# Attention feeding a gated feed-forward layer on one core: larger first loads, another order of the first unit, and the second normalisation beside two gate and value blocks

## The chip, the cores and the metric

The kernel runs on one core of a Trainium2 chip. A core has a matrix engine (TensorE, PE), a vector engine (VectorE, DVE), a scalar engine (ScalarE, ACT), GpSimd (POOL) and SyncE (SP), and 16 DMA engines that move data between the device memory and the on-chip memory. Each engine runs its own list of instructions in order and waits on semaphores of the others. The metric is the device time of one execution in microseconds.

## The reference

`q`, `k`, `v` are 8 batches x 12 heads x 448 positions x 64, in float32. The attention has no softmax: the scores are rectified and squared. Its result, 3584 tokens x 768, goes through a root-mean-square normalisation and a gated feed-forward layer of width 1536.

```python
scores = scale * np.matmul(q, k.transpose(0, 1, 3, 2))
attn = np.maximum(scores, 0.0) ** 2 / S
x = np.matmul(attn, v)                      # heads side by side: 3584 x 768
xn = x / np.sqrt(np.mean(x * x, axis=-1, keepdims=True) + 1e-06) * rms_g
g = xn @ w_gate
out = (g * (1.0 / (1.0 + np.exp(-g))) * (xn @ w_val)) @ w_out
```

## The kernel before

All matrix products are in bfloat16. The loads, issued by GpSimd, turn float32 into bfloat16 on the way. GpSimd keeps at most eight loads under way; a further one is issued when the one eight places ahead of it has landed.

A unit of attention is four heads of one batch, two pairs; a batch has three units (`ND = 3`), so unit `m` belongs to batch `m // 3`. For a unit, queries and keys are transposed so that the head dimension lies on the partitions (`QT`, `KT`). The keys of a pair come in three blocks of 128 (`NCH`) and a rest of 64 that both pairs share in one tile (`kx`, "late keys"); so a unit has seven score slots, 0 to 6. `scores` (line 318) makes the scores of a slot for both heads of a pair (TensorE), rectifies them (ScalarE, line 344) and squares them (VectorE, line 311). `attend` multiplies with the values into `psAV`, ScalarE scales the sums into `xT` and VectorE squares those into `xn`.

Batch 0 is done in two parts of its query positions, `US = ((0, 3), (3, 7))`: 192 and 256 positions. Its functions are `first_q`, `first_k` (transposes on TensorE, copies on VectorE, lines 255 and 277), `last_keys` (late keys), `part_scores` (line 351; four tiles a unit, slots (0,1), (2,3), (4,5), (6)), `part_attend` and `part_gates`. `late` collects the squares, to be issued afterwards (`flush`). From batch 2 on, the keys are transposed by DMAs that SyncE issues (`turn_by_dma`, line 285): three blocks and the late keys for a batch. Queries of batches 2 and 3 (`pr == 1`) are transposed by TensorE in `transposes` (line 190), from batch 4 on by DMA.

`norm` sums the squares over the model dimension by a product with ones (`psSS`), takes the root (ScalarE, line 492) and puts small VectorE steps on a list `bg`: two or four reciprocals (line 503), six scalings (line 506, one for each block of 128 of the model dimension), and last a call that makes the gate and value pieces available. `step()` does the next of these, `steps(n)` does n, `drain()` all. A piece on the list `pieces` is a block of products: for batch 0 the gate product of two column blocks (`psG`, line 530, followed by the sigmoid step `sig` on ScalarE, line 548) or the value product (`psV`, line 530, then the multiplication into `hT`, line 553). `piece(n)` runs the next n of them.

ScalarE loads a table of functions when it changes between the root and the sigmoid step (1.28 us each in the timeline). The PSUM memory is split into two buffers for scores (`psS`) and four that all other products share in turn (`rot`). `warm(k)` issues k products of ones with 448 columns (`psW`, line 303) whose result is not used; `warm_tile()` takes a buffer for them.

The opening is written out by hand, lines 138 to 168 for the loads and 679 to 747 for the work: first part of batch 0, its `norm`, second part with pieces of the first between, its `norm`, then the first slots of batch 1. From line 748 a loop over units takes over and fills with pieces by their costs; outputs follow from `outproj`.

Of the kernel before, what the change touches and what calls it, by code (L numbers as in the profile page):

```python
# [15 lines left out]
def kernel(  # L16
# [37 lines left out]
    def cols(h):  # L54
        return slice(US[h][0] * HALF, US[h][1] * HALF)
# [41 lines left out]
    def load_q0(h, h0=0, h1=H):  # L97

        u0, u1 = US[h]
        nc.gpsimd.dma_start(  # L100
            out=q_t[0][:HALF, h0:h1, u0:u1],
            in_=q[0, h0:h1].rearrange("h (p u) d -> p h u d", u=NU)[:, :, u0:u1],
        )
# [7 lines left out]
    def load_k(b, h0=0, h1=H):  # L111
        src = k[b, h0:h1, 0:XT0]
        form = "h (p c) d -> p h c d" if b < 2 else "h (p c) d -> p c h d"
        dst = k_t[b][:, h0:h1] if b < 2 else k_t[b][:]
        nc.gpsimd.dma_start(out=dst, in_=src.rearrange(form, c=NCH))  # L115

    def load_kx(b):
        nc.gpsimd.dma_start(out=kx_t[b][:], in_=k[b, :, XT0:S].rearrange("h p d -> p h d"))
# [19 lines left out]
    q_tile(0)  # L138
    k_tile(0)
    v_tile(0)  # L140
    load_q0(0, 0, 2)
    load_k(0, 0, 2)
    ident = const_pool.tile([P, P], BF16, name="ident", tag="ident")
    masks.make_identity(nc, ident[:])
    load_k(0, 2, 4)
    load_q0(0, 2, 12)
    load_k(0, 4, 8)
    load_kx(0)
    load_v(0, 0, 4)
    load_vx(0)  # L150
    load_k(0, 8, 12)
# [89 lines left out]
    def first_q(h, t, pairs=(0, 1)):  # L241

        u0, u1 = US[h]
        n, i0 = len(pairs), pairs[0]
        ps = psum.tile([P, n, u1 - u0, HALF], BF16, name="psQ", tag="rot", bufs=4)
        for i in pairs:
            for u in range(u0, u1):
                turn(
                    ps[:, i - i0, u - u0, :],
                    lambda hh: q_t[0][:, 4 * t + 2 * i + hh, u, :],  # L250
                    0,
                    HALF,
                )
        j = 2 * t + i0
        nc.vector.tensor_copy(out=QT[0][:, j : j + n, u0:u1, :HALF], in_=ps[:])

    def first_k(t, pairs=(0, 1)):

        w, n, i0 = (S if t else XT0), len(pairs), pairs[0]
        ps = psum.tile([P, n, w], BF16, name="psK", tag="rot", bufs=4)  # L260
        for i in pairs:
            for c in range(NCH):
                turn(
                    ps[:, i - i0, c * P : (c + 1) * P],
                    lambda hh: k_t[0][:, 4 * t + 2 * i + hh, c, :],
                    0,
                    P,
                )
            if t:
                turn(  # L270
                    ps[:, i, XT0:S],
                    lambda hh: kx_t[0][:, 4 * t + 2 * i + hh, :],
                    0,
                    XK,
                )
        j = 2 * t + i0
        nc.vector.tensor_copy(out=KTt[0][:, j : j + n, :w], in_=ps[:])
# [9 lines left out]
    def last_keys(m):  # L287

        b, t = divmod(m, ND)
        ps = psum.tile([P, 2, XK], BF16, name="psX", tag="rot", bufs=4)  # L290
        for i in range(2):
            turn(ps[:, i, :], lambda hh: kx_t[b][:, 4 * t + 2 * i + hh, :], 0, XK)
        nc.vector.tensor_copy(out=KTt[b][:, 2 * t : 2 * t + 2, XT0:S], in_=ps[:])
# [4 lines left out]
    def warm_tile():  # L298
        W["ps"] = psum.tile([P, S], FP32, name="psW", tag="rot", bufs=4)

    def warm(k):
        for _ in range(k):
            nc.tensor.matmul(  # L303
                out=W["ps"][:], lhsT=ones_bf[:, :P], rhs=ones_bf[:], start=True, stop=True
            )
# [45 lines left out]
    def part_scores(h, t, tiles, k=0, late=None):  # L351

        u0, u1 = US[h]
        w = (u1 - u0) * HALF
        qt, kt = QT[0], KTt[0]
        for x in tiles:
            warm(k)
            n = len(PARTS[x])
            ps = psum.tile([P, 2, 512], FP32, name="psS", tag="psS")
            for y, s in enumerate(PARTS[x]):  # L360
                if s < 2 * NCH:
                    i, c = divmod(s, NCH)
                    todo = [(2 * t + i, slice(0, P), slice(c * P, (c + 1) * P))]
                else:
                    todo = [
                        (2 * t + i, slice(i * XK, (i + 1) * XK), slice(XT0, S))
                        for i in range(2)
                    ]
                for j, rows, keys in todo:
                    for hh in range(2):  # L370
                        prt = slice(hh * D, (hh + 1) * D)
                        nc.tensor.matmul(  # L372
                            out=ps[rows, hh, y * w : (y + 1) * w].rearrange(
                                "k (u x) -> k u x", x=HALF
                            ),
                            lhsT=kt[prt, j, keys],
                            rhs=qt[prt, j, u0:u1, :HALF],
                            start=True,
                            stop=True,
                        )  # L380
            r = rpool.tile([P, 1024], BF16, name="r", tag="r")
            r = r[:, : 2 * n * w].rearrange("p (h x) -> p h x", h=2)
            nc.scalar.activation(out=r, in_=ps[:, :, : n * w], func=ACT.Relu)  # L383
            square(r, late)
            for y, s in enumerate(PARTS[x]):
                R[h, t, s] = r[:, :, y * w : (y + 1) * w]

    def part_attend(h, t):
        w = (US[h][1] - US[h][0]) * HALF
        acc = [psum.tile([P, w], FP32, name="psAV", tag="rot", bufs=4) for _ in range(2)]  # L390
        for s in range(2 * NCH + 1):
            r = R.pop((h, t, s))
            if s < 2 * NCH:
                i, c = divmod(s, NCH)
                todo = [(i, slice(0, P), v_t[0][:, 4 * t + 2 * i : 4 * t + 2 * i + 2, c])]
            else:
                c = NCH
                todo = [
                    (
                        i,  # L400
                        slice(i * XK, (i + 1) * XK),
                        vx_t[0][:, 4 * t + 2 * i : 4 * t + 2 * i + 2],
                    )
                    for i in range(2)
                ]
            for i, rows, v in todo:
                for hh in range(2):
                    nc.tensor.matmul(  # L408
                        out=acc[i][hh * D : (hh + 1) * D, :],
                        lhsT=v[rows, hh, :],  # L410
                        rhs=r[rows, hh, :],
                        start=(c == 0),
                        stop=(c == NCH),
                    )
        evacuate(0, t, [(slice(i, i + 1), acc[i][:]) for i in range(2)], cols(h))
# [245 lines left out]
    def piece(n=1):  # L661
        for _ in range(n):
            pieces.pop(0)[1]()

    def steps(n):
        for _ in range(n):
            step()
# [5 lines left out]
    def flush(late):  # L673
        while late:
            late.pop(0)()
# [1 line left out]
    N = B * ND  # L677
    late: list = []
    warm_tile()
    warm(8)  # L680
    big(0, 0)
    first_q(0, 0, (0,))
    first_k(0, (0,))
    warm(1)
    part_scores(0, 0, (0,), late=late)
    warm(2)
    first_q(0, 0, (1,))
    first_k(0, (1,))
    flush(late)
    part_scores(0, 0, (1, 2))  # L690
    last_keys(0)
    first_k(1)
    first_q(0, 1)
    part_scores(0, 0, (3,))
    warm_tile()
    for t in range(1, ND):
        part_scores(0, t, (0,))
        warm(1)
        part_scores(0, t, (1,))
        part_attend(0, t - 1)  # L700
        if t + 1 < ND:
            first_k(t + 1)
            first_q(0, t + 1)
            warm_tile()
        part_scores(0, t, (2, 3))
    first_q(1, 0)
    first_q(1, 1)
    warm_tile()
    warm(2)
    part_attend(0, ND - 1)  # L710
# [1 line left out]
    norm(0, cols(0), lambda: part_gates(0, (0, 2, 4, 6)))  # L712
    drain()
    warm_tile()
    part_scores(1, 0, (0, 1, 2, 3), 2)
    warm(7)
    warm_tile()
    piece(2)
    part_scores(1, 1, (0, 1))
    part_attend(1, 0)  # L720
    piece(1)
    part_scores(1, 1, (2, 3))
    first_q(1, 2)
    piece(1)
    part_scores(1, 2, (0, 1))
    part_attend(1, 1)
    piece(1)
    part_scores(1, 2, (2, 3))
    transposes(HP - 1)
    transposes(HP)  # L730
    last_keys(ND)
    piece(1)
    part_attend(1, 2)
    prefetch_v(0, ND - 1)
    transposes(HP + 1)
    warm_tile()
    warm(2)
    norm(0, cols(1), lambda: part_gates(1, (0, 2, 4, 6)))
    scores(ND, (0, 1), late=late)
    piece(1)  # L740
    steps(4)
    piece(1)
    scores(ND, (2, 3), late=late)
    drain()
    flush(late)
    for h in range(2):
# [60 lines left out]
```

## Time and profile before

| | us |
|---|---|
| median of 3 runs | 472.72 (472.03, 472.72, 484.08) |
| the profiled execution's own time | 475.79 |
| its span, first to last instruction | 474.0 |
| TensorE busy (97% of the span) | 459.7 |
| VectorE, ScalarE busy (54% each) | 254.1, 256.6 |
| GpSimd busy (14%) | 67.8 |

The difference between the profiled execution's own time and its span, 1.79 us, lies before the first and after the last instruction. TensorE's clock is granted in steps by the chip: the profile shows 1.00 or 0.50 of full speed. A busy TensorE at 0.50 does half as much. The loads of the opening, from the list of DMA issues with their times:

| load, heads | KB | issued | landed |
|---|---|---|---|
| queries 0-2 | 48 | 1.26 | 4.59 |
| keys 0-2 | 96 | 1.96 | 5.10 |
| keys 2-4 | 96 | 3.22 | 6.10 |
| queries 2-12 | 240 | 3.94 | 8.72 |
| keys 4-8 | 192 | 4.66 | 9.73 |
| late keys | 96 | 5.41 | 10.84 |
| values 0-4 | 192 | 6.17 | 11.70 |
| keys of batch 2 | 576 | 40.47 | 61.55 |

The KB are those that the profile gives (bytes as written).

### The profile page before, as it was taken

The page shows a single profiled execution, that of the slowest core. Times are in us where ns is not written, and L with a number is a line of the kernel's source. Part 1 is how long each engine was busy: PE and PEld are TensorE (multiplying, and loading weights), DVE is VectorE, ACT ScalarE, POOL GpSimd, SP SyncE. Part 2 cuts the span into 40 slices and gives each one's busy share as a digit, 9 for nine tenths or more (in the row PEclk, how much of TensorE's full clock was granted, in tenths as well). Part 3 has the DMA queues.
Part 4 walks back from the last instruction along what each step waited for, and adds up shares of the span by engine and source line. Part 5 has one row for each costly group of instructions (what it writes and reads, how often), then busy time and mean ns, then how long its engine had stood idle before and what let it go on. Part 6 is the DMA issues. An engine that isn't in the chain of part 4 may idle for free.

```text
span 474.0 us, 8047 instructions
## 1 busy us (share of the span) xinstructions
PE 459.7 (97%) x3276; PEld 240.7 (51%) x3276; DVE 254.1 (54%) x455; ACT 256.6 (54%) x378; POOL 67.8 (14%) x73
## 2 busy tenths in 40 slices
PE   6998899999999999999999999999999999999997
PEld 2556556654454454444445554444445555555564
DVE  2566777885448344955557435855566435522211
ACT  2567768955564567746565447646565444222111
POOL 9535210621040006100300002000000000000000
PEclk8579899999999999999999999999999999999999
DMA  9999999999999629920295548000001120000022
GB/s 100 195 195 192 183 157 130 179 124 133 44 126 183 174 73 132 147 36 1 26 119 134 140 121 88 2 0 1 1 17 68 66 84 2 0 1 0 35 100 100
DMA packets 134196, 42.79 MB, mean 90 GB/s; under 512 B 114576, under 2 KB 134160, under 8 KB 134160
## 3 DMA queue, kind: packets, MB, share of 16 engines
q0 software_dynamic: 97072, 24.38, 62.2%
q1 hardware_dynamic: 36944, 17.80, 17.5%
q8 instruction: 25, 0.41, 0.4%
q14 instruction: 11, 0.09, 0.1%
q10 hardware_dynamic: 144, 0.10, 0.1%
HBM read 48.76 MB, written 11.01 MB: 126 GB/s over the span
## 4 chain that ended last, share of the span: by engine, by line
PE 81%; DMA 6%; ACT 5%; DVE 5%; issue 2%; SPq 1%; POOL 1%; ACTq 0%; POOLq 0%
PE psO L617 21%; PE psG L575 20%; PE psV L589 20%; PE psS L335 6%; PE psAV L437 5%; DMA KT<-kld 4%; PE psW L303 2%; ACT r L344 2%; PE psSS L484 1%; PE psAV L408 1%; DVE r L311 1%; PE psS L372 1%; DMA out_dram<-ost 1%; ACT r L383 1%; DVE xn L506 1%
## 5 line engine op out<-in xcount | busy, mean ns | idle before, releaser
L311 DVE TENSOR_TENSOR r<-r 128x896 bf16<-128x896 bf16 (+4 forms) x171 | 103.9, 615 | 96.1 <-ACT r L344 87.5
L344 ACT ACTIVATE r<-psS 128x896 bf16<-128x896 f32 x147 | 128.0, 924 | 24.3 <-PE psS L335 24.2
L617 PE MATMUL psO<-wo_sb,hT 128*128 128x384 bf16 x672 | 113.2, 326 | 0.4 <-DVE hT L596 0.4
L575 PE MATMUL psG<-xn,wg_sb 128*128 128x448 bf16 x504 | 109.4, 353 | 0.2 <-DVE xn L506 0.2
L589 PE MATMUL psV<-xn,wv_sb 128*128 128x448 bf16 x504 | 109.2, 353 | 0.0
L583 ACT ACTIVATE sig<-psG 128x448 bf16<-128x448 f32 x84 | 45.7, 546 | 89.4 <-PE psG L575 87.2
L617 PEld LDWEIGHTS <-hT 128*128 128x128 bf16 x672 | 64.2, 98 | 47.0 <-issue 5.1
L596 DVE TENSOR_TENSOR hT<-sig,psV 128x448 bf16<-128x448 bf16 x84 | 51.7, 616 | 58.4 <-PE psV L589 56.9
L589 PEld LDWEIGHTS <-wv_sb 128*128 128x128 bf16 x504 | 47.9, 98 | 47.8 <-issue 4.9
L575 PEld LDWEIGHTS <-wg_sb 128*128 128x128 bf16 x504 | 48.0, 98 | 47.2 <-issue 4.0
L633 ACT COPY ost<-psO 128x384 f32<-128x384 f32 x28 | 13.4, 479 | 67.6 <-PE psO L617 50.4
L335 PE MATMUL psS<-QT,KT 64*128 64x448 bf16 (+1 forms) x336 | 44.8, 360 | 2.2 <-ACT r L344 1.8
L635 DVE COPY ost<-psO 128x384 f32<-128x384 f32 x27 | 15.0, 555 | 31.5 <-PE psO L617 31.4
L506 DVE SCALAR_TENSOR_TENSOR xn<-xT,g_sb,rstd 128x448 bf16<-128x448 bf16 (+2 forms) x54 | 31.5, 628 | 0.3
L121 POOL DMA_DIRECT2D vld<-in_v_dram x9 | 8.9, 986 | 156.4 <-PE psAV L437 154.4
L454 ACT ACTIVATE xT<-psAV 128x448 bf16<-128x448 f32 (+2 forms) x54 | 24.3, 503 | 10.3 <-PE psAV L408 5.4
L437 PE MATMUL psAV<-r,vld 128*64 128x448 bf16 x252 | 27.8, 357 | 0.0
L503 DVE RECIPROCAL rstd<-rstd 128x112 f32<-128x112 f32 (+2 forms) x32 | 25.0, 822 | 4.4 <-ACT rstd L492 4.4
L335 PEld LDWEIGHTS <-KT 64*128 64x128 bf16 (+1 forms) x336 | 11.6, 96 | 28.9 <-issue 27.3
L383 ACT ACTIVATE r<-psS 128x768 bf16<-128x768 f32 (+3 forms) x24 | 18.8, 830 | 13.7 <-PE psS L372 13.5
L455 DVE TENSOR_TENSOR xn<-xT 128x896 bf16<-128x896 bf16 (+2 forms) x27 | 15.5, 573 | 11.3 <-ACT xT L454 11.3
L115 POOL DMA_DIRECT2D kld<-in_k_dram x11 | 16.5, 1496 | 24.3 <-DMA KT<-kld 20.7
(53 smaller groups left out, 274.4 us busy)
## 6 DMA issues: line engine op xcount, KB each, us to landing
out_dram<-ost SPq DMA_DIRECT2D x55, 192.0 KB, 1.9
qld<-in_q_dram POOLq DMA_DIRECT2D x7, 672.0 KB, 20.1
kld<-in_k_dram POOLq DMA_DIRECT2D x7, 576.0 KB, 17.2
vld<-in_v_dram POOLq DMA_DIRECT2D x7, 576.0 KB, 7.0
wo_sb<-in_moe_w_out_dram POOLq DMA_DIRECT2D x3, 768.0 KB, 34.7
vxld<-in_v_dram POOLq DMA_DIRECT2D x16, 96.0 KB, 7.2
wg_sb<-in_moe_w_gate_dram POOLq DMA_DIRECT2D x4, 384.0 KB, 13.8
wv_sb<-in_moe_w_val_dram POOLq DMA_DIRECT2D x4, 384.0 KB, 15.0
```

The lines of the kernel that those rows point to most:

```text
L311: nc.vector.tensor_tensor(out=r, in0=r, in1=r, op=ALU.mult)
L335: nc.tensor.matmul(out=ps[rows, hh, :S].rearrange("k (u x) -> k u x", u=NU), lhsT=kt[prt, j, keys], rhs=qt[prt, j, :, b % 2 * HALF : (b % ...
L344: nc.scalar.activation(out=r, in_=ps[:, :, :S], func=ACT.Relu)
L437: nc.tensor.matmul(out=acc[i][hh * D : (hh + 1) * D, :], lhsT=w[rows, hh, :], rhs=r[rows, hh, :], start=(c == 0), stop=(c == NCH),)
L454: nc.scalar.mul(out=xt[:, i, sl], in_=acc, mul=inv_attn)
L503: nc.vector.reciprocal(out=rstd[:, cs], in_=rstd[:, cs])
L506: nc.vector.scalar_tensor_tensor(out=xn[:, kt, sl], in0=xt[:, kt, sl], scalar=g_sb[:, kt : kt + 1], in1=rstd[:, :w], op0=ALU.mult, op1=ALU ...
L575: nc.tensor.matmul(out=ps[:], lhsT=wg_sb[:, kt, fb * P : (fb + 1) * P], rhs=xn[:, kt, :], start=(kt == 0), stop=(kt == KT - 1),)
L583: nc.scalar.activation(out=sig[:, :S], in_=ps[:], func=ACT.Silu)
L589: nc.tensor.matmul(out=ps[:], lhsT=wv_sb[:, kt, fb * P : (fb + 1) * P], rhs=xn[:, kt, :], start=(kt == 0), stop=(kt == KT - 1),)
L596: nc.vector.tensor_tensor(out=HT[pr, fb][:, :, e * HALF : (e + 1) * HALF], in0=st["sig"][:, :S].rearrange("p (u x) -> p u x", u=NU), in1=p ...
L617: nc.tensor.matmul(out=ps[:], lhsT=HT[pr, fk][:, u, :], rhs=wo_sb[:, fk, o * OW : (o + 1) * OW], start=(fk == 0), stop=(fk == FT - 1),)
```

## The change

Three things change, all in the part written by hand. The first loads of queries and of keys take four heads each instead of two, the late keys are loaded third, and the remaining queries after keys 4 to 8. In the first unit all transposes of both pairs come first, then tiles 0 and 1 of the scores, then the late keys and tiles 2 and 3. In the first part two dummy products between tiles go, and all three `first_q(1, t)` are done at its end. Around the first `norm` there are fewer dummies, one tile of scores and one value piece stand in another order, and one gate and one value piece fewer run before the second `norm`, so that two pairs of them run behind it, among `steps`. The number of dummies falls from 42 to 39; all other TensorE instructions are the same in number.

```diff
-    load_q0(0, 0, 2)
-    load_k(0, 0, 2)
+    load_q0(0, 0, 4)
+    load_k(0, 0, 4)
     ident = const_pool.tile([P, P], BF16, name="ident", tag="ident")
     masks.make_identity(nc, ident[:])
-    load_k(0, 2, 4)
-    load_q0(0, 2, 12)
+    load_kx(0)
     load_k(0, 4, 8)
-    load_kx(0)
+    load_q0(0, 4, 12)
     load_v(0, 0, 4)
...
     warm_tile()
-    warm(8)
+    warm(10)
     big(0, 0)
-    first_q(0, 0, (0,))
+    first_q(0, 0)
     first_k(0, (0,))
+    first_k(0, (1,))
+    warm_tile()
+    part_scores(0, 0, (0,), late=late)
     warm(1)
-    part_scores(0, 0, (0,), late=late)
+    part_scores(0, 0, (1,), late=late)
+    last_keys(0)
+    flush(late)
     warm(2)
-    first_q(0, 0, (1,))
-    first_k(0, (1,))
-    flush(late)
-    part_scores(0, 0, (1, 2))
-    last_keys(0)
+    part_scores(0, 0, (2, 3))
     first_k(1)
     first_q(0, 1)
-    part_scores(0, 0, (3,))
     warm_tile()
+    warm(1)
     for t in range(1, ND):
-        part_scores(0, t, (0,))
-        warm(1)
-        part_scores(0, t, (1,))
+        part_scores(0, t, (0, 1))
         part_attend(0, t - 1)
...
-    first_q(1, 0)
-    first_q(1, 1)
+    for t in range(ND):
+        first_q(1, t)
     warm_tile()
     warm(2)
     part_attend(0, ND - 1)
...
     norm(0, cols(0), lambda: part_gates(0, (0, 2, 4, 6)))
     drain()
     warm_tile()
-    part_scores(1, 0, (0, 1, 2, 3), 2)
-    warm(7)
+    part_scores(1, 0, (0, 1), 2)
+    warm(1)
+    part_scores(1, 0, (2,), 2)
+    warm(1)
     warm_tile()
-    piece(2)
+    piece(1)
+    part_scores(1, 0, (3,))
+    piece(1)
     part_scores(1, 1, (0, 1))
     part_attend(1, 0)
     piece(1)
     part_scores(1, 1, (2, 3))
-    first_q(1, 2)
     piece(1)
     part_scores(1, 2, (0, 1))
     part_attend(1, 1)
-    piece(1)
-    part_scores(1, 2, (2, 3))
     transposes(HP - 1)
     transposes(HP)
+    part_scores(1, 2, (2, 3))
     last_keys(ND)
-    piece(1)
-    part_attend(1, 2)
-    prefetch_v(0, ND - 1)
     transposes(HP + 1)
     warm_tile()
     warm(2)
+    part_attend(1, 2)
+    prefetch_v(0, ND - 1)
+    warm(3)
     norm(0, cols(1), lambda: part_gates(1, (0, 2, 4, 6)))
     scores(ND, (0, 1), late=late)
     piece(1)
-    steps(4)
+    steps(2)
     piece(1)
-    scores(ND, (2, 3), late=late)
+    steps(2)
+    scores(ND, (2,), late=late)
+    piece(1)
+    steps(2)
+    scores(ND, (3,), late=late)
+    piece(1)
     drain()
```

## The prediction

> **What bounds the kernel now.** I read the page's slices first, then the busy time by stage, the timeline of TensorE's waits, and the chain in order of time.
>
> ```profile
> PE   6998899999999999999999999999999999999997
> ...
> PEclk8579899999999999999999999999999999999999
> DMA  9999999999999629920295548000001120000022
> GB/s 100 195 195 192 183 157 130 179 124 133 44 126 183 174 73 132 147 36 1 26 119 134 140 121 88 2 0 1 1 17 68 66 84 2 0 1 0 35 100 100
> ```
>
> A slice is 11.85 us. TensorE is full from slice 5 on; it is idle, or clocked below full, only in the first five. There the DMA engines are full too, near 195 GB/s. The busy time by stage sharpens this (columns: TensorE, weight loads, VectorE, ScalarE, GpSimd, granted clock, DMA share, GB/s):
>
> ```profile
> 0.00:8.30 8.30, 5.01 (x27) 1.79 (x27) 1.06 (x4) 2.09 (x2) 7.17 (x15) 1.00 0.74 71
> 8.30:28.80 20.50, 18.66 (x212) 10.59 (x213) 10.01 (x24) 10.47 (x18) 12.69 (x16) 0.50 1.57 191
> 28.80:56.10 27.30, 24.17 (x315) 16.21 (x314) 18.92 (x44) 21.46 (x32) 10.57 (x12) 1.00 1.62 191
> 56.10:59.50 3.40, 3.23 (x14) 1.91 (x14) 3.40 (x9) 1.69 (x3) 0.14 (x1) 0.50 1.97 176
> 59.50:83.80 24.30, 23.17 (x276) 14.64 (x275) 17.96 (x39) 18.82 (x27) 1.50 (x2) 1.00 1.54 144
> 83.80:474.00 390.20, 385.45 (x2434) 195.56 (x2434) 202.72 (x338) 202.04 (x299) 35.78 (x29) 1.00 0.65 74
> ```
>
> After 83.8 us TensorE idles 4.75 of 390 us: whatever moves the start of that stage moves the end by as much. Before it, TensorE idles 9.6 us (the differences of the first two columns) and has the clock at 0.50 for 23.9 us. The timeline shows the waits that the change touches, in brackets, and the last one before the full stage:
>
> ```profile
> 8.77 0.37 PE L190 MATMUL psQ<-ident,qld 64*64 64x64 bf16 x6 [1.98 <-DMA qld<-in_q_dram]
> ...
> 41.93 0.61 PE L372 MATMUL psS<-QT,KT 64*128 64x256 bf16 x8 [1.06 <-DVE QT L255]
> ...
> 54.60 0.25 PE L190 MATMUL psX<-ident,kxld 64*64 64x64 bf16 x4 [0.60 <-ACT sig L548]
> ...
> 60.19 1.47 PE L530 MATMUL psV<-xn,wv_sb 128*128 128x256 bf16 x12 [0.73 <-ACT sig L548]
> ...
> 83.82 0.55 PE L335 MATMUL psS<-QT,KT 64*128 64x448 bf16 x4 [0.25 <-DMA KT<-kld]
> ```
>
> The last is what I build on. At 83.82 the scores of the third batch need the third block of its transposed keys, which SyncE's transposing DMA brings. The chain goes through it:
>
> ```profile
> 63.00 2.38 SPq L285
> 65.38 0.05 issue
> 65.43 18.34 DMA KT<-kld
> 83.77 0.05 issue
> 83.82 0.55 PE psS L335 x4
> ```
>
> That DMA was issued at 65.43, behind the first two (61.64, 63.00), and the first waited for the key load that landed at 61.55. That load was issued at 40.47, as soon as the load eight places ahead of it on GpSimd's queue had landed (39.92): the loads keep a full queue, whatever TensorE does. So at this place TensorE already waits 0.25 us for the stream: being there earlier gains nothing by itself.
>
> **The change part by part.** U is the profiled execution: span 474.0, time 475.79, so 1.79 around it; the median is 472.72, 3.07 lower, and I carry that difference over unchanged.
>
> *First loads.* Query and key of four heads come in one load each, not two, and the late keys (kx) third. Now the first queries (48 KB) take 3.33 us from issue to landing, the 240 KB load 4.79: 7.6 ns per KB, so 96 KB issued at 1.26 land near 5.0. The first keys (96 KB) take 3.14; 192 KB behind others took 5.07 and 5.30. So the four heads' keys, issued near 1.98, land between 5.9 (3.14 plus 96 x 7.6 ns) and 7.3; I take 6.1, because the second 96 KB land at 6.10 today though issued 1.26 us later. The Trainium skill ("DMA: Bandwidth & Descriptors", Anatomy of one DMA) prices a GpSimd load at about 2 us plus its bytes over 436 GB/s; by that the doubling costs 0.2 us, an estimate, and the keys would land at 5.3.
>
> Two more dummy products at 0.37 us end at 5.1, under the wait for the keys. Then 12 + 12 transposes, the copies (0.35, 0.36, 0.36 on VectorE) and the first two scores run to about 7.5; the two ScalarE steps (0.81 and 0.76) gate the last two scores, which end near 9.3 against 13.1 now. The wait of 1.98 is gone; late next are the loads for the second unit: keys 4 to 8 and the rest of the queries, which with the same bytes ahead cannot be much before 10.8, when the kx load lands today. Eight key and twelve query transposes and their copies then lead to the next scores at about 12.0, against 13.52: 1.5 us.
>
> *First part.* Two dummies between scores go (0.49 each in the chain), sixteen query transposes come early (32 took 0.85 in the chain, so 0.43): 1.5 + 0.98 - 0.43 = 2.05 us ahead. Behind the first normalisation 8 dummies stand for 15; seven took 1.43 in the chain. The gate products may start 2.8 us after the sum of squares; the first scaled tile is there at 2.25, the sixth at 3.97, and its product, spaced at 0.27, comes at 4.15: covered by 0.2. Now 3.5 ahead. The 1.06 at 41.93 was for a copy of queries that is now early; next late there is ScalarE: two relu steps of about 0.95 must free the score buffers, some 0.5 us of wait. 4.3 ahead, less three dummies (0.6): 3.6 at the square root.
>
> *Second normalisation.* Two gate/value pairs, a piece each of about 1.0 us, run here, one pair more than now. On VectorE the first pair's products stand ahead of all six scalings; they wait for the sigmoid, which waits for two relus and the 1.28 us table load. So the last scaling is ready 7.4 us after the square root, not 5.66. TensorE has 2 us more to do meanwhile. Behind it waits the second part's first gate product, at about 52.9 instead of 56.71. The waits 0.60, 0.56, 0.44 shrink to about 1.3 in all, and if the clock holds, its 2.74 is about 1.48, as the next such product took. TensorE would then be 5.8 us ahead (4.5 if the clock falls as now), and reach the scores of 83.82 near 78.
>
> *What it meets.* The keys. Their transposes follow the load stream. Its start is filled sooner: from 2.65 to 6.5 us the queue's packets moved some 294 KB, and at 195 GB/s could have moved 750, a loss of 2.3 us. I bound the shift by 0 and 2.0 and take 0.8, a third, since single loads moved 90 to 100 KB per us and one issue of 0.74 is saved. The third key block then lands at 82.97 and the scores start at 83.02: 0.80 earlier, after a wait of about 5 us.
>
> *What the wait costs.* The clock fell at 56.1 after a 3.41 us window with no TensorE gap over 0.6 us, in which it was busy for 1.9; it stayed at 0.50 for one window. Five idle microseconds empty more than that. One window at 0.50 loses at most 1.7 us; 0.25 of wait at 100.21 can absorb some. Bounds 0 and 1.7, I take 1.2, nearer the row of 56.1. The Trainium skill ("TensorE: Matmul & The Clock Gate", Why this matters for your kernels) warns of gaps over about 3 us between bursts. This trace is stricter, the gaps before 56.1 being far shorter; by the rule alone a 5 us wait costs the window, and the sum would end 0.5 higher.
>
> Sum: 475.79 - 0.80 + 1.2 = 476.2; less 3.07: 473.1.
>
> **The rivals.**
>
> *The keys come early too* (0.27). For it: unprofiled runs are 3.07 us shorter, and if that is the DMA, TensorE is what was late at 83.82. Against it: the stream's 191 GB/s in both long stages. The gain is then what TensorE saved, 3.5 to 5.8: 466.9 to 469.2.
>
> *Slower: the cooled clock is not won back in one window* (0.15). The place is the stretch behind the scores of 83.0, whose transposes and 64-row scores did not win the clock back from 8.3 to 28.8, though TensorE was busy for 18.66 of 20.5 us. It decides if the wait passes 3.4 us and the next window isn't dense. Two windows lose 3.4; with a shift of 0 to 0.8: 475.3 to 476.1.
>
> *The opening does not start sooner* (0.08): the keys land at 7.3 or later, other queries bound the second unit, and the clock stays low as before. TensorE is 2 to 3 us ahead from the dummies alone, which the key wait takes: 0 to -0.8 without a cold window, 471.9 to 472.7.
>
> **How the numbers follow.** The forecast, 473.1, has 0.50; its own range is 470.7 (shift 2.0, no cold window) to 474.4 (no shift, a whole one). With the rivals the range is 467.0 to 476.1, which leaves out the top of the first rival. A difference of 2%, 9.5 us, is about what a measurement of this kernel can tell from no change. Faster by that needs more than all TensorE can save here: 0.04. Slower by it needs the load stream itself to lose 9 us: 0.06. Within: 0.90.
>
> **What would show it.** The first query wait of 1.98 gone; the scores of the second unit at about 12; the gate product of the second part near 53; then the wait for KT<-kld before the third batch's scores grown from 0.25 to 3 to 5.5 us, ending near 83, and a stage at clock 0.50 behind it. Wrong, if that wait stays under 1 us with the scores well before 82, or if the key load lands more than 2 us off 60.8.

## The result, and the profile after

The changed kernel takes 471.69 us (median of 12 runs, 469.23 to 481.48), the kernel before, on the same chip, 474.72 (12 runs, 472.03 to 484.9). The ratio is 0.9938, interval 0.9909 to 0.9968: some 2.9 us shorter, where the forecast saw no change (+0.4). The change is well inside 2%, but the interval leaves out 1.000, and four later comparisons on other chips gave 0.9933, 0.9935, 0.9936 and 0.9936. The profiled execution took 471.86, its span is 470.1. (Some executions are disturbed, over 1.5% longer than the fastest of their kernel; the ratios leave them out, and of the profiled executions that of e12, 481.35, is one and is used only where it is named.)

The same four rows of the page's 40 slices, now of the changed kernel:

```profile
PE   7898899999999999999999999999999999999997
...
PEclk9799999999999999999999999999999999999999
DMA  9999999999697549910596447000002110000022
GB/s 107 196 194 193 182 171 107 192 144 131 31 164 179 143 102 131 121 34 1 56 112 140 131 124 70 2 0 1 1 17 83 70 68 1 1 1 0 35 100 100
```

TensorE is a little fuller in the first slice, the transfers look the same, and the clock row shows only one fall, in the second slice. The busy time by stage (columns as before), cut at the clock's steps and at the two places that the prediction names:

```profile
0.00:18.50 18.50, 13.44 (x178) 7.01 (x178) 8.69 (x22) 9.75 (x17) 14.99 (x24) 1.00 1.30 139
18.50:25.40 6.90, 6.62 (x78) 4.23 (x79) 2.46 (x6) 2.27 (x5) 2.96 (x4) 0.51 1.45 197
25.40:55.20 29.80, 25.74 (x309) 16.60 (x308) 20.86 (x48) 23.84 (x34) 11.91 (x14) 1.00 1.59 192
55.20:79.60 24.40, 23.17 (x276) 14.64 (x275) 19.37 (x42) 19.00 (x27) 1.49 (x2) 1.00 1.70 143
79.60:470.10 390.50, 385.29 (x2434) 195.59 (x2434) 202.05 (x337) 201.46 (x298) 35.73 (x29) 1.00 0.67 76
```

The last stage, from the third batch's scores on, is 390.5 us long against 390.2 before: the gain is made ahead of it. The clock is at 0.50 for 6.9 us there, not 23.9. The timeline of TensorE's waits:

```profile
18.78 1.49 PE L189 MATMUL psQ<-ident,qld 64*64 64x64 bf16 x48 [1.05 <-DMA qld<-in_q_dram]
...
38.68 0.41 PE L189 MATMUL psQ<-ident,qld 64*64 64x64 bf16 x14 [0.96 <-DMA qld<-in_q_dram]
...
52.76 1.71 PE L529 MATMUL psG<-xn,wg_sb 128*128 128x256 bf16 x12 [0.40 <-DVE hT L552]
...
55.21 1.47 PE L529 MATMUL psV<-xn,wv_sb 128*128 128x256 bf16 x12 [0.73 <-ACT sig L547]
...
79.62 0.55 PE L334 MATMUL psS<-QT,KT 64*128 64x448 bf16 x4 [1.03 <-ACT xT L453]
```

The first query wait (1.98) is gone. Two waits for later query loads have come, 1.05 and 0.96: TensorE is now early enough to meet them. At the scores of the third batch, where the prediction has TensorE wait 5 us until about 83, it waits 1.03 until 79.62. The timeline puts this down to ScalarE, and so does the chain in order of time (start, length, what):

```profile
79.07 0.55 ACT xT L453
79.62 0.00 issue
79.62 0.55 PE psS L334 x4
```

That ScalarE step, `xT`, is not one that these scores need. ScalarE's timeline of the kernel before, where they start at 83.82, shows it still running then:

```profile
83.61 0.98 ACT L454 ACTIVATE xT<-psAV 128x448 bf16<-128x448 f32 x2
```

By the list of transfers the third key block of the changed kernel lands at 79.57. These scores wait for that landing too, and they start 0.05 us behind it, as they do in the kernel before (83.77 and 83.82) and, below, in e16 and e17. So the 1.03 us is the predicted wait for the keys, at a fifth of its predicted length.

From the second part's first value product (55.21) to these scores it is 24.41 us; before, from 60.19 to 83.82, it was 23.63. So 0.8 of the lead goes here, where the forecast has all but 0.8 of it go.

In the following table the leads are the start of an instruction in the kernel before (first profile) less its start in the changed kernel. Columns A to E are five profiled executions of the unaltered changed kernel: the first one and the controls e4, e11, e13, e18.

| start of | before | forecast lead | A | B | C | D | E |
|---|---|---|---|---|---|---|---|
| scores of the second unit | 13.52 | 1.5 | 2.17 | 1.99 | 1.74 | 1.47 | 0.62 |
| first part's sum of squares | 27.77 | 2.05 | 3.46 | 3.35 | 4.28 | 2.45 | 1.34 |
| second part's sum of squares | 49.50 | 3.6, and two pieces moved behind it, 2.0 | 5.90 | 6.38 | 4.91 | 6.43 | 4.70 |
| second part's first value product | 60.19 | 5.8; 4.5 if the clock falls | 4.98 | 4.74 | 3.58 | 5.51 | 3.78 |
| batch 1's first gate product (L574) | 98.82 | -0.4 | 4.46 | 3.15 | 3.58 | 5.51 | 3.78 |
| end of the span | 474.0 | -0.4 | 3.9 | 3.1 | 3.1 | 5.6 | 3.6 |

From L574 to the end all twenty profiles of this study take 374.3 to 376.0 us, so what moves that product moves the end.

### The profile page after: what moved, and what is told of

Its sections match the earlier page's. It is cut to its first block, busy times and chain, and to the rows that moved or that the text cites. A ratio compares the mean times of both kernels' runs of the same rounds, so it can differ in the third digit from the quotient of the medians.

```text
span 470.1 us, 8042 instructions
## 1 busy us (share of the span) xinstructions
PE 454.3 (97%) x3273; PEld 238.1 (51%) x3273; DVE 253.4 (54%) x454; ACT 256.3 (55%) x378; POOL 67.1 (14%) x72
## 4 chain that ended last, share of the span: by engine, by line
PE 81%; DMA 7%; ACT 4%; DVE 4%; POOL 2%; issue 1%; ACTq 0%; POOLq 0%
PE psO L616 22%; PE psG L574 20%; PE psV L588 20%; PE psS L334 7%; PE psAV L436 6%; DMA qld<-in_q_dram 4%; DMA wg_sb<-in_moe_w_gate_dram 2%; ACT r L343 2%; PE psG L529 2%; PE psV L529 1%; PE psSS L483 1%; DVE xn L505 1%; DMA out_dram<-ost 1%; DVE rstd L502 1%; PE psQ L189 1%
## 5 line engine op out<-in xcount | busy, mean ns | idle before, releaser
L574 PE MATMUL psG<-xn,wg_sb 128*128 128x448 bf16 x504 | 109.4, 353 | 0.2 <-DVE xn L505 0.2
L574 PEld LDWEIGHTS <-wg_sb 128*128 128x128 bf16 x504 | 48.0, 98 | 47.2 <-issue 4.0
L436 PE MATMUL psAV<-r,vld 128*64 128x448 bf16 x252 | 27.8, 357 | 0.0
L382 ACT ACTIVATE r<-psS 128x768 bf16<-128x768 f32 (+3 forms) x24 | 18.5, 829 | 9.9 <-PE psS L371 9.8
L436 PEld LDWEIGHTS <-vld 128*64 128x64 bf16 x252 | 12.5, 109 | 13.8 <-issue 7.5
```

The lines of the kernel that those rows point to most:

```text
L436: nc.tensor.matmul(out=acc[i][hh * D : (hh + 1) * D, :], lhsT=w[rows, hh, :], rhs=r[rows, hh, :], start=(c == 0), stop=(c == NCH),)
L574: nc.tensor.matmul(out=ps[:], lhsT=wg_sb[:, kt, fb * P : (fb + 1) * P], rhs=xn[:, kt, :], start=(kt == 0), stop=(kt == KT - 1),)
```

## The experiments

Each ratio is to runs of the kernel before that were taken beside it on the same chip; their medians on the five chips lie between 474.65 and 475.14 us.

**Does the landing of the keys bind, and do both kernels repeat?** e1 is the kernel before and e4 the changed kernel, with no edit.

> The kernel before, unchanged, for a second profile. Theory A (the load stream sets when batch 3's predecessor, batch 2, gets its third key block, and the change moved that landing): the key load of batch 2 lands at 61.5 +- 0.5 us and the third transposed block near 83.8 +- 0.7 again; ratio 1.000 +- 0.004. Theory B (the landing is scatter from run to run, and the gain of the change is TensorE's order): the third block lands anywhere from 79 to 84 in this profile.

> The changed kernel, unchanged, for a second profile. Theory A: key load of batch 2 near 59.9, third block at 79.6 +- 0.7, a wait of about 1 us there; ratio 0.994 +- 0.003. Theory B: third block anywhere from 79 to 84, the wait between 0 and 5 us with it.

Measured: e1 0.9988 (0.9962 to 1.0013), e4 0.9933 (0.9904 to 0.9962). In e1 the same program's third key block lands at 75.37, not 83.77, and the span is 474.1, as it was. Two lines of e1's list of transfers for the tile of the transposed keys between 55 and 70 us (the three transposing DMAs with their issue times; time from issue to landing, over these three and that of the late keys):

```profile
L285 SPq DMA_TRANSPOSE KT<-kld x3: 1304/2541/3091, 59.5 to 63.4; - x3
...
DMA to landing us min/median/max: 9.8/11.0/12.0
```

In the profile that the prediction was made from, the slowest of the three took 18.34 us. TensorE comes to these scores in e1 when it is ready, with nothing in brackets behind the line:

```profile
83.29 0.38 PE L437 MATMUL psAV<-r,vxld 64*64 64x448 bf16 x4
83.61 0.62 PE L335 MATMUL psS<-QT,KT 64*128 64x448 bf16 x4
```

83.61 against 83.82: the keys had come 8 us before. That TensorE and the keys met within 0.25 us in the first profile was chance. In e4 the block lands at 74.58 and there is no wait either.

**Which part of the change makes the gain?** e2 and e10 have the loads alone, e3 all but the loads. The loads' edit, against the kernel before:

```diff
-    load_q0(0, 0, 2)
-    load_k(0, 0, 2)
+    load_q0(0, 0, 4)
+    load_k(0, 0, 4)
...
-    load_k(0, 2, 4)
-    load_q0(0, 2, 12)
+    load_kx(0)
     load_k(0, 4, 8)
-    load_kx(0)
+    load_q0(0, 4, 12)
```

> The changed loads alone, TensorE's order as before. Theory A: the key load of batch 2 lands near 60 and the third block near 80 to 81, but TensorE gets there only 1 to 2 us earlier than 83.6, so the time falls by 1 to 2 us and the wait for KT<-kld is gone. Theory B: the time falls by what TensorE gains in the first unit, about 1 us, and the landings are the same as before within scatter.

> All of the change but the loads, which are as before. Theory A: the key load of batch 2 lands at 61.5, the third block near 83.8, TensorE waits 2 to 4 us there, and the time is that of before within 1.5 us (ratio 0.997 to 1.004). Theory B: TensorE's order makes the gain; time 2 to 3 us below before (ratio 0.994 to 0.996), wait under 1 us.

> The changed loads alone, once more, since four runs were too few. Theory C: the first unit's order is made for the old loads, with the second pair's transposes behind two dummies, so only a part comes: the second unit's scores near 13.2 us instead of 14.0, ratio 0.995 to 0.999. Rival G (the loads alone do it): ratio 0.991 to 0.994.

Measured: e2 gave too few runs for a ratio (profiled 473.47), e10 0.9979 (0.9955 to 1.0003), e3 1.0024 (0.9997 to 1.0052). The new order with the old loads needs the queries of the second pair at once and waits for them, longer than the kernel before did. Timeline of e3:

```profile
9.24 0.37 PE L190 MATMUL psQ<-ident,qld 64*64 64x64 bf16 x6 [3.64 <-DMA qld<-in_q_dram]
```

e5 and e15 have the loads, the first unit and the first part as changed, and the second part with its normalisation as before; e9 is the reverse, with all three `first_q(1, t)` at the end of the first part as in the change. The edit of e5 and e15, against the changed kernel:

```diff
-    for t in range(ND):
-        first_q(1, t)
+    first_q(1, 0)
+    first_q(1, 1)
...
-    part_scores(1, 0, (0, 1), 2)
-    warm(1)
-    part_scores(1, 0, (2,), 2)
-    warm(1)
+    part_scores(1, 0, (0, 1, 2, 3), 2)
+    warm(7)
...
```

> The changed loads with the changed first unit and first part; from the first drain on as before. Theory C (the two parts of the change add up in TensorE's time; the landing of batch 2's keys binds in none of the runs on a chip where it is at 75 us): the sum of squares of the first part starts near 24.4 us as with the whole change, the scores of the second part's third unit near 38.5, and the time is 2 to 3.5 us below before (0.993 to 0.996). Theory D (only the rework around the second part gains, the opening's lead is taken back by the loads): the query transposes of batch 1, near 39 to 40 us, wait and the time is that of before within 1 us.

> Old loads, old first unit and first part (with the third query transposition of the second part moved into it, as in the change), and the changed order from the first drain on. Theory C (the gain is made by the loads with the first unit; the rework of the second part is worth nothing): the sum of squares of the first part starts near 28 us as before, from there to the first value product of the second part TensorE takes no less than before plus the 2 us of the pair that is moved there; ratio 0.998 to 1.002. Rival F (the rework gains 2 us by itself, as forecast, and only the loads hid it): ratio 0.993 to 0.997.

> Changed loads, first unit and first part; the second part and its normalisation as before the change. Theory 'the rework of the second normalisation is worth nothing': within 0.6 us of the control, 0.991 to 0.995, or below it by the query wait that it does not have. Rival 'it is worth the 2.2 us of the forecast': 2 us above the control, 0.996 to 0.999.

Measured: e5 0.9911 (0.9877 to 0.9944, 4 runs), e15 0.995 (0.9924 to 0.9976, 12 runs) beside 0.9936 of the unaltered changed kernel on e15's chip; e9 0.9989 (0.9958 to 1.0019). The loads together with the order of the first unit and part carry most of the gain. Neither the loads alone (e10) nor all the rest without them (e3) shows one. The second part's rework is worth some 1 us by the medians of the undisturbed runs (472.81 in e15, 471.77 beside it), and the intervals of e15 and e9 allow for nothing as well as for about 2.

**Is the gain given back at the queries of batch 1, or at the clock?** e6 and e14 are the changed kernel with the third quarter of the gate and value weights loaded later, e12 is e5 with the same edit; e7 has six dummies more (two at the end of each turn of the unit loop, two ahead of the last transposes), e8 both edits. The edit of e6, against the changed kernel:

```diff
-    load_gv(512, 768)
...
     load_q(0, (1,))
+    load_gv(512, 768)
```

> The changed kernel with the third quarter of the gate and value weights loaded after batch 1's queries instead of before its keys; the same bytes. Theory C: the queries of batch 1 land near 34.5 instead of 38.2 to 38.6, the wait there (0.3 to 1.0 us) is gone; time 0.3 to 1.0 us below the changed kernel, ratio to before 0.991 to 0.993. Theory E (the wait is slack that a later wait takes anyway): ratio as the changed kernel, 0.993 to 0.994, with the wait turning up at the values' product near 41 or at the sigmoid near 55.

> The changed kernel with six more unused products where TensorE waits in the first part (two near 15 us, four near 17.7, ahead of the wait for the queries' second part). If the clock sets the pace of the opening, it stays at 1.00 to 25 us instead of falling at 15.5 or 18.5; the sum of squares then starts near 22.5 instead of 24.4, but the query transposes of batch 1 wait for their load near 38.2, so the time stays within 0.7 us of the changed kernel. If the clock does not follow from such products, it falls as before and the time is 0.3 to 1 us above the changed kernel.

> Both edits together. Theory C with the clock: what the products gain is no longer taken by the load; time 1.5 to 2.5 us below the changed kernel, ratio to before 0.988 to 0.991. If either the clock does not follow or a later load (third key block of batch 2) takes it: as the changed kernel, 0.992 to 0.995.

> The loads and the first unit and part of the change, the second part as before, and the third quarter of the gate and value weights loaded after batch 1's queries. Theory C: no wait for batch 1's queries in either version of the second part, so this is as fast as the better of the two: ratio 0.988 to 0.991, at or below the changed kernel in the same runs. Rival H (the second part's rework is worth 1 us or more): slower than the changed kernel with the same load order, which had 0.987.

> Changed kernel with the third quarter of the gate and value weights loaded behind the queries of batch 1 instead of ahead of them. Theory 'the wait for these queries is part of what the change gives back' (0.29 to 1.98 us in three profiles of the changed kernel): the wait is gone and the time is 0.3 to 1.9 us below the control of the same chip, 0.987 to 0.991 of before. Rival 'the 0.9874 measured before was that chip': the same as the control within 0.5 us, about 0.993.

Measured: e6 0.9874 (0.9834 to 0.9913, 4 runs), e14 0.9939 (0.9911 to 0.9968) beside 0.9936 of its control, e12 0.9956 (0.9921 to 0.9991), e7 0.9912 (0.9876 to 0.9947), e8 0.9902 (0.9866 to 0.9938). The low ratio of e6 did not come again. All four kernels of its chip (e5 to e8) have low ratios, and no unaltered changed kernel ran beside them, so these four are not to be set against 0.9936. e7 shows how one loss replaces another: its clock stays at 1.00 from 6.5 to 37.2 us, and the queries then cost more than in A. Timeline of e7:

```profile
37.89 0.58 PE L189 MATMUL psQ<-ident,qld 64*64 64x64 bf16 x14 [2.39 <-DMA qld<-in_q_dram]
```

**The unaltered changed kernel beside other edits.**

> The changed kernel on this chip, for comparison: ratio 0.993 +- 0.003. Theory C: the third key block of batch 2 lands before TensorE needs it, or makes it wait by less than 1.5 us.

> The changed kernel unaltered, beside the two that follow. All theories: 0.990 to 0.995 of before, as in the comparisons so far (0.9938, 0.9933, 0.9935); the third key block of batch 2 lands before TensorE asks for it or at most about 1 us after.

> The changed kernel unaltered, control for the two beside it: 0.993 to 0.994, the table load behind the sum of squares again, the root 2.4 to 2.5 us after the sum's start.

Measured: 0.9935 (0.9913 to 0.9957), 0.9936 (0.9910 to 0.9961), 0.9936 (0.9905 to 0.9967). The clock falls at other times in each. Its row in D (e13):

```profile
PEclk8599999999999999999999999999999999999999
```

D runs the opening at 0.50 from 8.0 to 25.0 us and still has the shortest span of the five, 468.4: it arrives late enough to meet no wait for the queries. Up to L574, TensorE is busy 89.14 and idle 9.68 us in the kernel before. In A it is busy 83.71 and idle 10.65: the clock and three dummies fewer give 5.4, waits take 1.0. In D it is busy 86.45 and idle 6.86: both give, 2.7 and 2.8.

**Why is the second normalisation's rework worth so little?** The forecast gave it 2.2 us, of which 1.26 were to come from the second part's first gate product at full clock. Timeline of TensorE, of the kernel before:

```profile
56.71 2.74 PE L530 MATMUL psG<-xn,wg_sb 128*128 128x256 bf16 x12
```

and of e15, which has the second part as before:

```profile
54.05 1.48 PE L529 MATMUL psG<-xn,wg_sb 128*128 128x256 bf16 x12
56.27 1.47 PE L529 MATMUL psV<-xn,wv_sb 128*128 128x256 bf16 x12 [0.73 <-ACT sig L547]
```

So the old order has this product at 1.48 too, where the clock holds. From the second sum of squares to the first value product the old order takes 10.69 and 10.63 us in the two profiles of the kernel before, in which the clock falls at 56, and 9.23 or 9.24 in e2, e5, e10 and e15, in which it does not. The new order takes 11.61 in A, D and E, and in e9, with two pieces more, which take 2.09 in e15 (48.26 to 50.35): 9.52. At equal clock the rework of this stretch cost 0.3 us. A part of the reason is on ScalarE. Its timeline around the square root, of the kernel before:

```profile
48.69 0.66 ACT L454 ACTIVATE xT<-psAV 128x256 bf16<-128x256 f32 x2 [2.04 <-PE psAV L408]
49.36 1.28 ACT L492 ACT_TABLE_LOAD   x1
50.66 0.47 ACT L492 ACTIVATE rstd<-psSS,eps_col 128x256 f32<-128x256 f32 x1
```

and of the changed kernel:

```profile
44.76 1.28 ACT L491 ACT_TABLE_LOAD   x1 [0.97 <-PE psSS L483]
46.05 0.47 ACT L491 ACTIVATE rstd<-psSS,eps_col 128x256 f32<-128x256 f32 x1
```

Before, the table of the square root is loaded beside the sum of squares; in the changed kernel its load waits 0.97 for the end of the sum. The sums start at 49.50 and 43.60, so the root comes 1.16 us behind the sum's start in the one and 2.45 in the other. In the trace of the changed kernel the wait for TensorE's semaphore sits on the table load, and the root itself waits for ScalarE's own earlier work; before, the load has no wait, and the wait for TensorE sits on the root. e16 and e17 put a square root of one column, which nobody reads, ahead of the sum; e17 has e14's load edit too.

```diff
+    one_root = const_pool.tile([P, 1], FP32, name="one_root", tag="one_root")
...
+    nc.scalar.activation(out=one_root[:], in_=eps_col[:], func=ACT.Sqrt)
     warm(3)
     norm(0, cols(1), lambda: part_gates(1, (0, 2, 4, 6)))
```

> Changed kernel with one more ScalarE instruction, a square root of one column into a tile that nobody reads, ahead of the second norm. In the changed kernel ScalarE loads the square root's table only after the sum of squares (44.76, behind a wait of 0.97), in the kernel before already ahead of it (49.36): 1.28 us more on the way to the scalings. Theory 'this exposed table load eats what the reworked second normalisation saves': the table is loaded before the sum, the root follows 1.2 us after the sum's start instead of 2.45, TensorE's waits of 0.18, 0.27 and 0.40 before the second part's first gate product and 0.2 of that product's 1.71 go, up to 1.2 us, and the time is 0.7 to 1.3 us below the control, 0.990 to 0.9925 of before. Rival 'TensorE's own work sets that stretch': the root is early, but the gate product comes no more than 0.3 us sooner after the sum, the time as the control's, 0.9935.

> The same with the third quarter of the gate and value weights behind the queries of batch 1 (so the wait for these cannot take the gain). Theory of the table load: 0.990 to 0.9925, as the run beside it; if the queries' wait of batch 1 counts in the common run, up to 0.5 us lower than it. Rival: 0.9935.

Measured: e16 0.991 (0.9878 to 0.9942), e17 0.9909 (0.9878 to 0.994), the unaltered one beside them 0.9936. The medians of their undisturbed runs are 470.01, 470.60 and 471.17. ScalarE's timeline of e16:

```profile
44.45 1.28 ACT L738 ACT_TABLE_LOAD   x1
45.74 0.20 ACT L738 ACTIVATE one_root<-eps_col 128x1 f32<-128x1 f32 x1
45.85 0.46 ACT L492 ACTIVATE rstd<-psSS,eps_col 128x256 f32<-128x256 f32 x1
```

The load starts 0.2 us behind the sum's start (44.25) and waits for nothing; the root comes 1.60 behind that start. From the sum's start to the second part's first gate product it is 8.29 us (52.54) against 9.16 in the control: 0.87 less, as the theory of the table load expected (up to 1.2). e17 has 8.30, and A, B and D have 9.16. So with the early root the rework of this stretch (10.74 in all, less 2.09, against 9.23) gains about 0.6 us at equal clock, where it cost 0.3. The gain in time, 0.0026 of 474.9 or 1.2 us, agrees with it, but the intervals of e16 and its control overlap, and e17's median is only 0.6 below the control's; the 0.87 rests on the traces, the 1.2 is not shown. Both runs also show what the prediction had expected everywhere. Timelines of e16 and of e17 at the third batch's scores:

```profile
80.05 0.55 PE L335 MATMUL psS<-QT,KT 64*128 64x448 bf16 x4 [1.68 <-DMA KT<-kld]
```

```profile
81.53 0.93 PE L335 MATMUL psS<-QT,KT 64*128 64x448 bf16 x4 [4.06 <-DMA KT<-kld]
```

In these two executions the keys land at 80.01 and 81.48. Behind e17's 4.06 us the clock is at 0.50 from 80.4 to 87.2, and that execution, 476.14, is longer than any of the other undisturbed runs of its kernel (469.47 to 471.07).

## Why the prediction was wrong

**The step that failed** is "being there earlier gains nothing by itself", with the third key block put at 82.97. It took the landing of one execution for a property of the program. Besides the first profile, with 0.25, there are nineteen: fourteen have it at 73.9 to 76.6 us, one at 77.8; TensorE comes to these scores between 77.5 and 85. Time is lost only where the block is late: at 79.57 (A, a wait of 1.03), 80.01 (e16, 1.68), 81.48 (e17, 4.06), and at 87.96 in e12's disturbed execution (7.17). Elsewhere TensorE goes on without a wait of over 0.1, and what it saved before moves the end. In the five executions of the changed kernel no wait at this place is over 1.03, although TensorE came to L574 3.2 to 5.5 us earlier. The evidence was in reach: e1, the same program once more, would have shown it, and so would the question why the third of three equal transfers took 18.34 us and the first 9.79.

**The rival "the keys come early too"** had the mechanism, and was given a chance of 0.27. Its gain of 3.5 to 5.8 was too large for the runs, 2.9, though it fits the profiles: spans 3.1 to 5.6 shorter, 3.9 in the mean. The difference is in the kernel before: both of its profiled executions have a mean clock of 0.975, and of 86 undisturbed runs of it the 36 below 0.98 have a median of 475.96, the 18 from 0.98 to 0.99 473.3 and the 32 above 474.2. (A run whose clock records begin late counts as 1.00 until then, so these means sort the runs only roughly.) The profile showed its long form. For the same reason the 3.07 us that the prediction carried over were too many: the larger sets of runs have medians 0.6 to 1.1 below 475.79.

**First loads and first unit**: queries landed at 4.35 and keys at 5.68 (5.0 and 6.1 forecast), the second unit's scores started at 11.35 to 12.90 (12.0). Right; the loads came some 0.5 us sooner than forecast.

**First part**: forecast 2.05 ahead at the first sum, measured 1.3 to 4.3, 3.0 in the mean. What was mis-sized is the clock, which the prediction left as it was; A, B and C keep 1.00 until 15.5 to 18.5 us and have 3.3 to 4.3; D and E, at 0.50 for most of it, have 2.45 and 1.34.

**Square root**: 3.6 ahead for equal work, measured 5.66 in the mean, less 2.0 for the two pieces: 3.66. Right, but by another way: more came from the opening, and 0.96, 0.29 and 1.98 us (A, B, C) went at the queries of batch 1, a wait that no step of the prediction has. The steps of the sum itself do not add up by some 0.2: 2.05 and 1.43, and 1.06 less 0.5, make 4.0 where it has 4.3, and 3.4 where it has 3.6. That the number fits is in part luck.

**Second normalisation**: forecast 2.2, measured 0.9 (4.52 in the mean at the value product, against 3.66). The terms that it names make 1.6: waits shorter by 0.3, and 1.26 for the gate product. The 1.26 came in part (2.74 before, 1.71 in A, 1.48 forecast), but it is the clock's and not the rework's, as e15 shows. The other 0.6 has no term. It would need most of the wait for the sigmoid ahead of the value product to go, and that is 0.73 before, in A and in e15. From the sum to the gate product the forecast implies 9.0 us (from 43.9, which is 49.50 less 3.6 and 2.0, to 52.9), and 9.16 came; there the early root has 0.87 more to give. The 7.4 us to the last scaling, counted like the 5.66 from the root's end, were 6.98 in A (46.52 to 53.50), but the root came 1.3 later behind the sum, for which the prediction has no term. The Trainium skill ("ScalarE: Activation LUTs", What ACT_TABLE_LOAD costs) puts a change of tables at 2.66 us, a load of 1.28 and a drain of 1.38; in this trace the root starts 0.01 us behind the load's end, so here only the 1.28 is seen.

**TensorE's lead near 55 us**, 5.8 or 4.5 with the cold clock: 3.6 to 5.5, 4.5 in the mean. The size is nearly right; it was then not given back.

**The cooled clock behind the wait**: forecast 1.2 (0 to 1.7). It exists, in the one undisturbed profile with such a wait, and is larger: from the second part's first value product to L574 it is 44.8 us in e17 and 39.8 in e16, of which the longer wait is 2.4 and so the clock some 2.6, two windows and not one. The Trainium skill ("TensorE: Matmul & The Clock Gate", Why this matters for your kernels) warns of gaps over about 3 us; the 4.06 agree with that. The fall at 53.1 in e4 does not: no wait in the 3.4 us before it is over 0.40, and TensorE is busy for 2.51 of 3.50.

**What stays open**: whether e6's later weights help (0.9874 once, 0.9939 beside its control); whether the second part's rework as a whole is worth anything without the early root (0 to 2 by the intervals); why the clock falls near 56 us in the kernel before and not in e2, e5, e10 and e15, which have the same order there; and what a kernel would gain that keeps the clock and has the queries early at once, which no profile showed.

## What to carry to other kernels

Before a forecast rests on "that transfer lands at 83.8", ask for a second execution, and look whether equal transfers took equal time: a wait of 0.25 us between two streams may be a meeting by chance. When an order is changed, look at where the function-table loads fall: a load that stood beside other work can come to stand behind a wait, at its full length. The engine that is full for 390 us is not helped there; the place to shorten is the stretch in which it is idle or clocked down.

## What the runs showed of the hardware

The third key block's time goes steeply with the time at which the key load before it lands. In the twenty profiles: key load at 58.2 to 59.6, the block takes 10.6 to 13.5 us from its issue; at 59.8 to 60.4, 14.1 to 15.7; at 60.9 to 61.6, 16.1 to 18.3, and 22.4 in e12's disturbed execution. Three microseconds in the one go with five to eight in the other, so that the block lands up to ten later. The loads of the output weights that GpSimd issues at 58.7 to 62.8 run beside these blocks; that they are the reason was not tried.

The clock's phase is not the program's: five executions of the unaltered changed kernel have it at 0.50 from 18.5, 15.5 (and 53.1), 16.1 (and 40.0), 8.0 and, in E, from before the first record to 27.8. In E the page says 1.00 for that time, because nothing is recorded, but six key transposes take 0.53 us as in D at 0.50, against 0.36 in A at 1.00. The duration of a known product tells the clock where the clock's row cannot.
